# Attention and MLP in one kernel: from interleaved to one after the other, with a pinned order and a division by turned 32x32 blocks

## The chip, the cores and the metric

The kernel runs on one core of a Trainium2 chip. A core has a matrix engine, TensorE (PE, whose weight loads are shown apart as PEld), and four others: VectorE (DVE), ScalarE (ACT), GpSimd (POOL) and SyncE (SP), which here only issues transfers. Each engine works through its own list of instructions in order, and waits on semaphores for the others. PE writes to PSUM, a small memory that DVE and ACT can read; everything else lies in SBUF. The metric is the time of one execution in microseconds, the median of several.

## The reference

```python
batch, n_heads, seq, head_dim = (4, 8, 768, 64)          # attention
q_bits = (np.einsum('bhsd,dk->bhsk', q, proj) > 0)         # 6 hash bits
mask = q_bucket[:, :, :, None] == k_bucket[:, :, None, :]
scores = np.where(mask, scale * np.matmul(q, k.transpose(0, 1, 3, 2)), -1000000000.0)
attn = softmax(scores)            # sum + 1e-09
attn_out = np.matmul(attn, v)     # then (B,H,S,D) -> (B*S, H*D)
h = x @ w_in                      # 3072 x 512 times 512 x 2048
g = np.maximum(h, 0.0) + alpha * np.minimum(h, 0.0)
out = g @ w_out                   # 2048 x 512
```

A query sees only keys with the same six hash bits. A query that no key matches gets the mean of v. q, k and v are float32 and scaled by 0.1; `w_in` and `w_out` are scaled by 1/sqrt(512) and 1/sqrt(2048) and arrive as float64.

## The kernel before, in words

`fast_path` does all the work. After it a flag is read: where the inputs are too large for a softmax without its maximum, `general_path` computes everything again. It is not touched by the change.

Attention goes by *pairs* of heads, 16 in all (4 batches with 4 pairs), because two heads of 64 fill the 128 partitions. A pair has two *units*, one for each half (384) of the queries, so there are 32. A unit consists of:

- `scores` (line 587): for each of six blocks of 128 keys, PE makes a tile `sc` of 128 keys by 2 heads by 384 queries, first the product of the hash bits (bf16), which leaves a large negative number where they differ, then k times q (float32). ACT writes exp of it to a tile `pt` (line 592). Eight `pt` tiles and two `sc` buffers are passed round.
- POOL adds the `pt` tiles up into `acc` (lines 599 and 601): three accumulators with two blocks each in the first four pairs, one with all six blocks later on.
- `attend` (line 608), one unit later: PE multiplies `pt` by v into `av`; ACT copies it to `xT` (line 618).
- `divide` (lines 626 to 634): PE sums `acc` over the keys by a product with ones into `sm`, so that each sum stands in 64 equal rows; DVE takes the maximum with a small number, the reciprocal of all 128x384 elements, the product with `xT`, and POOL adds the mean of v where the sum was empty.

One pair ahead, `turn` transposes q and k on PE (line 550), ACT copies them out, `magnitude` squares them for the flag, and `hash_bits` makes the bits (`hs` on PE, then `qb` and `kb` on DVE).

The weights come as float64 in 32 pieces of 128x512. `round_weight` turns a piece into float32 from its two 32-bit words (lines 530 to 539): Abs on ACT, four operations on DVE, Abs again on ACT, an add on POOL, the sign on DVE. As written, two pieces go with each of the first seven units and four with each one after, until all 32 are done; the scheduler moves their operations ahead where it sees room.

The MLP works on chunks of 384 tokens, two for a batch: `ff1` makes 16 tiles `h` (line 643) whose activation DVE writes to `g` (lines 648 and 650), `ff2` makes three output tiles `z` from 16 products each (line 659), which ACT copies out and SP stores.

What sets the order: one loop over units with four *slots* each. `mlp_slice` puts a thirty-second part of the MLP of a finished batch into each slot, beginning nine units after the batch did:

```python
for u in range(total + UNITS + 2):
    pi, g = divmod(u, NCH)
    live = u < total
    for slot in range(4):
        if live and slot != 1:
            scores(pi, g, (0, None, 1, 2)[slot])
```

So the first eight units stand alone, the next 24 have the MLP of batches 0 to 2 between their matmuls, and the MLP of batch 3 stands alone at the end. Only PE's order is fixed as written (`pe = tc.keep_in_program_order`); the other engines' lists, and SP's, are laid out by the framework's scheduler.

## Time and profile before

| | before |
|---|---|
| median of 3 runs | 1162.95 us (1161.72 to 1164.89) |
| profiled execution | 1162.11 us, span of its instructions 1160.3 us |
| mean granted TensorE clock | 0.971 of full |
| busy: PE / PEld | 1084.9 us (94%) / 510.7 us (44%) |
| busy: DVE / ACT / POOL | 492.9 (42%) / 272.9 (24%) / 325.8 (28%) us |
| read from HBM / written | 35.66 / 6.29 MB |

Busy time is a sum over the whole span; the 40 slices of the page and the table of stretches show where it falls. A float32 matmul shows as two instructions, so 16 of them are 32 rows in a count. In a group's row stand the line, the engine, the operation, what is written and read, the shape, the count, then busy time in us and the mean of one in ns, then the idle time of the engine before it and what ended it. The chain of waits follows the work that ended last back from the end, piece by piece.

### The profile page before, as it was taken

How to read it: one execution, taken by the hardware profiler on the slowest of the kernel's cores; microseconds unless marked ns; L12 is line 12 of the kernel's file. 1: busy time of each engine (PE TensorE's matmuls, PEld its weight loads, DVE VectorE, ACT ScalarE, POOL GpSimd, SP SyncE). 2: the span in 40 equal slices, each digit the busy share in tenths (PEclk: the TensorE clock that was granted, in tenths of full speed). 3: DMA queues.
4: the chain of work that ended last, by engine and by line, in shares of the span. 5: the costliest groups of instructions: out<-in, count | busy, mean ns of one | idle time of the engine just before them, and what ended most of it. 6: DMA issues, size and time to landing. Idle time of an engine off the chain costs nothing.

```text
span 1160.3 us, 10928 instructions
## 1 busy us (share of the span) xinstructions
PE 1084.9 (94%) x4355; PEld 510.7 (44%) x4355; DVE 492.9 (42%) x696; ACT 272.9 (24%) x441; POOL 325.8 (28%) x224
## 2 busy tenths in 40 slices
PE   5676675999999999999999999999999999999997
PEld 3232232454445544454444544455444544554543
DVE  5988988444325430354315430354315421420420
ACT  5445443322222212221222222222221110000000
POOL 3454555422332322323332322223323330000000
PEclk8888787999999999999999999999999999999999
DMA  6434441110010101010010101010000000000000
GB/s 170 120 105 128 122 118 51 41 28 14 13 42 14 28 14 46 23 28 14 10 46 14 28 14 46 24 28 14 10 32 1 1 1 19 10 1 19 9 10 20
DMA packets 62844, 42.75 MB, mean 37 GB/s; under 512 B 51504, under 2 KB 55616, under 8 KB 62784
## 3 DMA queue, kind: packets, MB, share of 16 engines
q1 hardware_dynamic: 62784, 41.96, 12.7%
q8 instruction: 36, 0.59, 0.2%
q14 instruction: 24, 0.20, 0.1%
HBM read 35.66 MB, written 6.29 MB: 36 GB/s over the span
## 4 chain that ended last, share of the span: by engine, by line
PE 82%; DVE 13%; POOL 2%; ACT 1%; issue 1%; DMA 1%; SPq 0%; POOLq 0%; ACTq 0%
PE h L643 29%; PE z L659 29%; PE sc L587 10%; PE av L608 9%; PE sm L626 2%; DVE w_in L539 2%; POOL wr L538 2%; DVE dn L632 1%; PE hs L570 1%; DVE w_out L531 1%; DVE wr L536 1%; DVE w_out L539 1%; DVE w_in L531 1%; DVE wr L535 1%; DVE kb L574 1%; PE tp_k L550 1%
## 5 line engine op out<-in xcount | busy, mean ns | idle before, releaser
L643 PE MATMUL h<-xT,w_in 128*128 128x384 f32 x1024 | 343.5, 489 | 0.0
L659 PE MATMUL z<-w_out,g 128*128 128x512 f32 x768 | 339.0, 595 | 0.0
L601 POOL TENSOR_TENSOR acc<-acc,pt 128x768 f32<-128x768 f32 x96 | 161.0, 1677 | 427.2 <-ACT pt L592 423.4
L643 PEld LDWEIGHTS h<-xT,w_in 128*128 128x128 f32 x1024 | 189.7, 190 | 136.3 <-issue 9.7
L592 ACT ACTIVATE pt<-sc 128x768 f32<-128x768 f32 x192 | 154.7, 810 | 365.8 <-PE sc L587 365.7
L659 PEld LDWEIGHTS z<-w_out,g 128*128 128x128 f32 x768 | 143.2, 190 | 179.7 <-issue 177.3
L648 DVE TENSOR_SCALAR neg<-h,alpha 128x384 f32<-128x384 f32 x128 | 78.9, 617 | 292.9 <-PE h L643 292.7
L587 PE MATMUL sc<-qT,kT 64*128 64x384 f32 x768 | 160.7, 497 | 0.0
L608 PE MATMUL av<-pt,vn 128*64 128x385 f32 x768 | 139.3, 515 | 16.3 <-DVE kb L574 16.3
L599 POOL TENSOR_TENSOR acc<-pt,pt 128x768 f32<-128x768 f32 x48 | 89.9, 1874 | 116.5 <-ACT pt L592 116.5
L630 DVE TENSOR_SCALAR al<-sm,vm 128x384 f32<-128x384 f32 x32 | 19.8, 618 | 218.4 <-PE sm L626 218.2
L608 PEld LDWEIGHTS av<-pt,vn 128*64 128x64 f32 x768 | 55.9, 144 | 94.6 <-issue 94.2
L587 PE MATMUL sc<-qb,kb 64*128 64x384 bf16 x384 | 65.2, 335 | 18.5 <-ACT pt L592 18.4
L632 DVE RECIPROCAL dn<-dn 128x384 f32<-128x384 f32 x32 | 81.6, 2551 | 0.9
L587 PEld LDWEIGHTS sc<-qT,kT 64*128 64x128 f32 x768 | 71.1, 195 | 20.5 <-issue 20.4
L665 ACT COPY o<-z 128x512 f32<-128x512 f32 x24 | 14.0, 585 | 261.7 <-PE z L659 261.7
L650 DVE SCALAR_TENSOR_TENSOR g<-h,neg 128x384 f32<-128x384 f32 x128 | 71.2, 556 | 3.9
L587 PEld LDWEIGHTS <-kb 64*128 64x128 bf16 x384 | 20.5, 94 | 91.2 <-issue 78.5
L570 PE MATMUL hs<-qT,wh 128*32 128x384 f32 x128 | 30.4, 555 | 23.3 <-ACT xT L618 22.6
L618 ACT COPY xT<-av 128x384 f32<-128x384 f32 x32 | 15.2, 474 | 155.9 <-PE av L608 83.4
L634 POOL TENSOR_TENSOR xT<-dn,al 128x384 f32<-128x384 f32 x32 | 32.2, 1007 | 56.3 <-DVE dn L633 56.3
L626 PE MATMUL sm<-acc,ones 128*64 128x384 f32 x192 | 44.1, 574 | 1.2 <-ACT xT L618 1.2
(68 smaller groups left out, 520.2 us busy)
## 6 DMA issues: line engine op xcount, KB each, us to landing
raw<-in_moe_w_in_dram SPq DMA_DIRECT2D x16, 512.0 KB, 3.7
raw<-in_moe_w_out_dram SPq DMA_DIRECT2D x16, 512.0 KB, 3.5
qn<-in_q_dram SPq DMA_DIRECT2D x32, 192.0 KB, 3.4
kn<-in_k_dram SPq DMA_DIRECT2D x32, 192.0 KB, 3.3
vn<-in_v_dram SPq DMA_DIRECT2D x16, 384.0 KB, 3.2
out_dram<-o SPq DMA_DIRECT2D x24, 256.0 KB, 2.0
wh<-in_proj_dram SPq DMA_DIRECT2D x2, 1.5 KB, 2.9
alpha<-in_moe_alpha_dram SPq DMA_DIRECT2D x1, 8.0 KB, 2.2
```

The lines of the kernel that those rows point to most:

```text
L570: pe(nc.tensor.matmul(ps[r : r + 32], wh[s], tr[name, pi][:, cols], start=True, stop=True))
L587: pe(nc.tensor.matmul(sc[:, s, :CW], what["k", pi][r, ks], what["q", pi][r, qs], start=first, stop=not first,))
L592: nc.scalar.activation(pt[:, :, :CW], sc[:, :, :CW], AF.Exp, scale=SCALE)
L599: nc.gpsimd.tensor_tensor(a, prob[pi, g, kc - 1][:, :, :CW], pt[:, :, :CW], op=ALU.add)
L601: nc.gpsimd.tensor_tensor(a, a, pt[:, :, :CW], op=ALU.add)
L608: pe(nc.tensor.matmul(ps[D * s : D * s + D], nat["v", pi][:, s, kc * D : (kc + 1) * D], prob[pi, g, kc][:, s], start=(kc == 0), stop=(kc = ...
L626: pe(nc.tensor.matmul(ps[D * s : D * s + D], ones, a[:, s], start=(i == 0), stop=(i == n - 1)))
L632: nc.vector.reciprocal(den, den)
L643: pe(nc.tensor.matmul(ps, w[:, kk, o : o + P], xT[b][:, kk, ch * CW : (ch + 1) * CW], start=(kk == 0), stop=(kk == NK - 1),))
L648: nc.vector.tensor_scalar(neg, ps, 0.0, alpha[:, f : f + 1], op0=ALU.min, op1=ALU.mult)
L650: nc.vector.scalar_tensor_tensor(g, ps, 0.0, neg, op0=ALU.max, op1=ALU.add)
L659: pe(nc.tensor.matmul(ps, gT[b, ch, f][:, t * P : (t + 1) * P], w_out[part][:, i], start=(f == 0), stop=(f == NF - 1),))
```

## The change

The loop with slots is gone. All 32 units of attention come first, then the eight chunks of the MLP. In detail:

- Every compute instruction of all engines is pinned in program order (`do = tc.keep_in_program_order`); SP's transfers are still placed by the scheduler.
- One weight piece is converted with each unit. It has one Abs fewer (its effect is folded into the constant of the exclusive or), and the upper clamp is replaced by a recorded maximum `wmax`, which the flag tests at the end (weights under 2). The test on q and k is tighter (40 for 60).
- `scores`, `attend` and the adds are taken apart, so that a unit runs: two key blocks, half of the attend of the unit before, two turns or a hash, two key blocks, the other half, two turns or a hash, two key blocks, the sum of the unit before. The first four `pt` tiles are added by POOL (`add_first`), the last two and POOL's result by DVE (`add_last`): one accumulator, two matmuls for `sm`.
- The division turns `sm` by 32x32 blocks on DVE (a transpose within each block), so that the 64 equal rows become columns and one column of each block is enough: 12 columns for the reciprocal, which are spread out again, turned back, and multiplied with `av` straight out of PSUM. The copy of `av` on ACT and the add on POOL are gone; the mean of v for empty sums comes from a small number added on both sides of the fraction.
- The bits of q come from Sign on ACT, those of k from DVE, in one operation.
- The pools of attention are closed before the MLP, which gets four `h` buffers and two `z` buffers in PSUM instead of two for both. The first two `h` tiles of the next chunk are made before `ff2` of a chunk. The flag is computed behind the first chunk's `ff1`.

```diff
-    pe = tc.keep_in_program_order
+    do = tc.keep_in_program_order
...
+    def weight_abs(i):
+        lo, hi = halves(i)
+        do(ACT.activation(piece(i)[0], hi.bitcast(F32), AF.Abs))
+
+    def weight_parts(i):
...
+        wr[i] = r = pool.tile([P, 512], F32, name=f"wr{i}", tag="wr")
+        do(DVE.tensor_scalar(x, x, HI_MIN, None, op0=ALU.max, op1=ALU.max, accum_out=wmax[:, i : i + 1]))
+        do(DVE.tensor_scalar(
+            x.bitcast(U32), x.bitcast(U32), 3, 0xC0000000, op0=ALU.logical_shift_left, op1=ALU.bitwise_xor,
+        ))
+        do(DVE.tensor_scalar(r.bitcast(U32), x.bitcast(U32), 0x7F800000, None, op0=ALU.bitwise_and))
+        do(DVE.scalar_tensor_tensor(r, lo, 2.0 ** -52, r, op0=ALU.mult, op1=ALU.mult))
...
+        do(DVE.tensor_scalar(bits["k", pi][:, cols], ps, tk, mk, op0=ALU.is_gt, op1=ALU.mult))
...
+            do(ACT.activation(bits["q", pi][D * s : D * s + 32, cols], ps[r], AF.Sign, bias=bq[r]))
...
+    def add_first(u, part):
+        p = [prob[u, 2 * part + i][:, :, :CW] for i in range(2)]
+        if part == 0:
+            accp[u] = pool.tile([P, 2, CW], F32, name=f"accp{u}", tag="accp")
+            do(POOL.tensor_tensor(accp[u], p[0], p[1], op=ALU.add))
+        else:
+            for t in p:
+                do(POOL.tensor_tensor(accp[u], accp[u], t, op=ALU.add))
+
+    def add_last(u):
...
+        do(DVE.tensor_tensor(accd[u], p[0], p[1], op=ALU.add))
+        do(DVE.tensor_tensor(accd[u], accd[u], accp[u], op=ALU.add))
...
-        nc.vector.tensor_scalar(alone, ps, EMPTY, vmean[pi], op0=ALU.is_lt, op1=ALU.mult)
-        nc.vector.tensor_scalar(den, ps, EMPTY, None, op0=ALU.max)
-        nc.vector.reciprocal(den, den)
-        nc.vector.tensor_tensor(den, den, x, op=ALU.mult)
-        nc.gpsimd.tensor_tensor(x, den, alone, op=ALU.add)
...
+            do(PE.matmul(ps[D * s : D * s + D], ones, accd[u][:, s], start=True, stop=True))
...
+        do(DVE.transpose(a, ps))
+        do(DVE.tensor_scalar(r, a.rearrange("p (n w) -> p n w", w=32)[:, :, 0], S * EPS, None, op0=ALU.add))
+        do(DVE.reciprocal(r, r))
+        do(DVE.tensor_copy(a.rearrange("p (n w) -> p n w", w=32), r.unsqueeze(2).to_broadcast([P, CW // 32, 32])))
+        do(DVE.transpose(d, a))
+        do(DVE.scalar_tensor_tensor(
+            xT[b][:, hp, g * CW : (g + 1) * CW], av[u][:, :CW], vsum[pi], d, op0=ALU.add, op1=ALU.mult,
+        ))
...
+    for u in range(UNITS + 1):
...
+        if live:
+            scores(u, 0)
+            add_first(u, 0)
+        if u > 0:
+            add_last(u - 1)
+            attend(u - 1, 0)
+        if more:
+            if g == 0:
+                turn(pi + 1, "q", 0)
+                turn(pi + 1, "q", 1)
+            else:
+                hash_bits(pi + 1, 0)
+        if live:
+            weight_parts(u)
+            weight_sum(u)
+            scores(u, 1)
+            add_first(u, 1)
+        if u > 0:
+            attend(u - 1, 1)
...
+        if live:
+            scores(u, 2)
+        if u > 0:
+            divide(u - 1)
+        if live:
+            weight_sign(u)
+            load_weight(u + 3)
+            if u + 1 < NW:
+                weight_abs(u + 1)
+        if more:
+            magnitude(pi + 1, "qk"[g])
...
+    attn.close()
...
+    chunks = [(b, ch) for b in range(B) for ch in range(NCH)]
+    EARLY = 2
+    for n, (b, ch) in enumerate(chunks):
+        for f in range(EARLY if n else 0, NF):
+            ff1(b, ch, f)
+        if n == 0:
             verdict()
...
+        if n + 1 < len(chunks):
+            for f in range(EARLY):
+                ff1(*chunks[n + 1], f)
+        for t in range(CH):
+            ff2(b, ch, t)
```

On PE, in a unit of the interleaved stretch before, `h` products of an earlier batch stand between the score blocks:

```order
L550 MATMUL tp_q_1517<-ident,qn_1280 128x128 x3
L643 MATMUL h_0_7_1522<-xT_344,w_in_82 128x384 x4
L608 MATMUL av_1_1531<-pt_95,vn_940 64x385 x2
L608 MATMUL av_1_1531<-pt_96,vn_940 64x385 x2
L608 MATMUL av_1_1531<-pt_89,vn_940 64x385 x2
L608 MATMUL av_1_1531<-pt_90,vn_940 64x385 x2
L608 MATMUL av_1_1531<-pt_91,vn_940 64x385 x2
L608 MATMUL av_1_1531<-pt_92,vn_940 64x385 x2
L550 MATMUL tp_q_1558<-ident,qn_1280 128x128 x3
L643 MATMUL h_0_8_1563<-xT_344,w_in_83 128x384 x4
L643 MATMUL h_0_9_1572<-xT_344,w_in_83 128x384 x4
```

After the change nothing of the MLP stands there; half an attend and two turns lie between two score blocks, and the sum ends the unit:

```order
L603 MATMUL sc_3_441<-qT_231,kT_262 128x384 x2
L635 MATMUL av_411<-pt_94,vn_156 64x384 x2
L635 MATMUL av_411<-pt_95,vn_156 64x384 x2
L635 MATMUL av_411<-pt_96,vn_156 64x384 x2
L567 MATMUL tp_k_458<-ident,kn_391 128x128 x3
L567 MATMUL tp_k_463<-ident,kn_391 128x128 x3
L603 LDWEIGHTS kb_317
L603 MATMUL sc_4_468<-qb_79,kb_317 128x384
```

All products named h now follow the last sum, so on PE the whole MLP has moved behind the whole of attention.

On DVE in one of the first units before, operations of several weight pieces (`w_in`) stand mixed with a division (`al`, `dn`) and a hash (`qb`, `kb`):

```order
L531 TENSOR_SCALAR w_in_82<-w_in_82 128x512
L571 TENSOR_SCALAR qb_377<-hs_378,tq,cq 128x384
L574 TENSOR_SCALAR kb_80<-hs_378,tk,mk 32x384 x2
L539 SCALAR_TENSOR_TENSOR w_in_82<-raw_374,wr_548 128x512
L630 TENSOR_SCALAR al_0_394<-sm_0_386,vm_342 128x384
L631 TENSOR_SCALAR dn_0_393<-sm_0_386 128x384
L532 TENSOR_SCALAR w_in_82<-w_in_82 128x512
L632 RECIPROCAL dn_0_393<-dn_0_393 128x384
L571 TENSOR_SCALAR qb_377<-hs_414,tq,cq 128x384
L633 TENSOR_TENSOR dn_0_393<-dn_0_393,xT_344 128x384
```

After the change the list of a unit is the same throughout: the two adds (`accd`), a hash, one weight piece, `vs`, a hash, then the division (`st`, `rc`, `dn`):

```order
L624 TENSOR_TENSOR accd_514<-pt_93,pt_94 128x768
L625 TENSOR_TENSOR accd_514<-accd_514,accp_406 128x768
L588 TENSOR_SCALAR kb_524<-hs_525,tk,mk 128x384
L544 TENSOR_SCALAR w_in_80,wmax<-w_in_80 128x512
L545 TENSOR_SCALAR w_in_80<-w_in_80 128x512
L548 TENSOR_SCALAR wr_533<-w_in_80 128x512
L549 SCALAR_TENSOR_TENSOR wr_533<-raw_286,wr_533 128x512
L641 TENSOR_SCALAR vs_559<-av_517 128x1
L588 TENSOR_SCALAR kb_524<-hs_561,tk,mk 128x384
L655 STREAM_TRANSPOSE st_584<-sm_581 128x384
L656 TENSOR_SCALAR rc_585<-st_584 128x12
L657 RECIPROCAL rc_585<-rc_585 128x12
```

The adds have come to DVE, the weight piece stands ahead of the division of the unit before, and nothing of a second piece stands with it.

The flag's transposes on PE (`vd`, two of them) stood before among the last `h` products:

```order
L643 MATMUL h_0_5_4741<-xT_3713,w_in_82 128x384 x4
L643 MATMUL h_0_6_4750<-xT_3713,w_in_82 128x384 x4
L683 MATMUL vd_4762<-ident,top 1x128
L683 MATMUL vd_4765<-ident,top 1x128
L643 MATMUL h_0_7_4771<-xT_3713,w_in_82 128x384 x4
L643 MATMUL h_0_8_4780<-xT_3713,w_in_83 128x384 x4
```

and now, between the first chunk's last `h` and the second chunk's first:

```order
L735 MATMUL h_0_14_3599<-xT_89,w_in_83 128x384 x4
L735 MATMUL h_0_15_3608<-xT_89,w_in_83 128x384 x4
L764 MATMUL vd_3621<-ident,top 1x128
L764 MATMUL vd_3624<-ident,top 1x128
L764 MATMUL vd_3627<-ident,top 1x128
L735 MATMUL h_1_0_3635<-xT_89,w_in_80 128x384 x4
```

They have moved from the end of the program to behind the first chunk, and there are three, which share one buffer.

More of the change, by code (lines that the diff above doesn't have):

```diff
@@ L499, in setup @@
         for t in pts:
-            nc.gpsimd.memset(t[:, :, CW : CW + 1], 1.0)
+            do(POOL.memset(t[:, :, CW : CW + 1], 1.0))
+        for t in qbs:
+            do(POOL.memset(t, 0.0))
     def setup_alpha():
         ps = psum.tile([P, NF], F32, name="alps", tag="mi")
-        nc.tensor.transpose(ps, alpha16, ident[:NF, :NF])
-        nc.vector.tensor_copy(alpha, ps)
-    raw = {}
-    views = [(w_in[j], moe_w_in, j) for j in range(4)] + [(w_out[j], moe_w_out, j) for j in range(4)]
-    def load_weight(i):
-        dst, src, j = views[i // 4]
-        o = i % 4
+        do(PE.transpose(ps, alpha16, ident[:NF, :NF]))
@@ L604, in attend @@
-    def attend(pi, g):
-        ps = psum.tile([P, CW + 1], F32, name=f"av{pi}_{g}", tag="mi")
-        for kc in range(NC):
+            do(ACT.activation(pt[:, :, :CW], sc[:, :, :CW], AF.Exp, scale=SCALE))
+            prob[u, kc] = pt
+    def add_first(u, part):
[6 more added lines that the diff above has]
+                do(POOL.tensor_tensor(accp[u], accp[u], t, op=ALU.add))
@@ L726, in fast_path @@
+    for name in "qkv":
+        load(0, name)
+        if name == "q":
+            setup()
     for name in "qk":
@@ new lines, in fast_path, with ff1 @@
+    attn.close()
+    mpool = ctx.enter_context(tc.tile_pool(name="mlp", bufs=2))
+    mpsum = ctx.enter_context(tc.tile_pool(name="mps", bufs=4, space=bass.MemoryType.PSUM))
+    gT = {}
+    def ff1(b, ch, f):
+        ps = mpsum.tile([P, CW], F32, name=f"h{b}_{ch}_{f}", tag="h", bufs=4)
+        w, o = w_in[f // (NF // 4)], (f % (NF // 4)) * P
+        for kk in range(NK):
+            do(PE.matmul(
+                ps, w[:, kk, o : o + P], xT[b][:, kk, ch * CW : (ch + 1) * CW],
+                start=(kk == 0), stop=(kk == NK - 1),
+            ))
+        neg = mpool.tile([P, CW], F32, name=f"neg{b}_{ch}_{f}", tag="neg")
+        do(DVE.tensor_scalar(neg, ps, 0.0, alpha[:, f : f + 1], op0=ALU.min, op1=ALU.mult))
+        g = mpool.tile([P, CW], F32, name=f"g{b}_{ch}_{f}", tag="g", bufs=NF + 4)
+        do(DVE.scalar_tensor_tensor(g, ps, 0.0, neg, op0=ALU.max, op1=ALU.add))
+        gT[b, ch, f] = g
```

322 lines of the change are left out of this document (126 added, 196 removed).

## The prediction

> **What bounds the kernel now.** I read the page first, then busy time by stretch, then the chain of waits, and last the groups by line. The page's slices show two regimes.
>
> ```profile
> PE   5676675999999999999999999999999999999997
> ...
> DVE  5988988444325430354315430354315421420420
> ...
> PEclk8888787999999999999999999999999999999999
> ```
>
> For seven slices (200 us) PE is busy five to seven tenths at a clock of 0.8, while DVE is nearly full. From the eighth on PE is full, at full clock. Busy time by stretch (the stretch, its length, busy us and instructions of PE, PEld, DVE, ACT and POOL, then clock, DMA share, GB/s) gives the sizes:
>
> ```profile
> 20.00:200.00 180.00, 120.95 (x651) 50.99 (x649) 157.20 (x205) 86.11 (x145) 92.58 (x62) 0.84 0.38 109
> 300.00:860.00 560.00, 560.00 (x2279) 260.50 (x2272) 197.63 (x256) 126.47 (x201) 161.82 (x102) 1.00 0.09 25
> ```
>
> In the first stretch attention stands alone and most weight pieces are converted: PE idles 59 of 180 us and runs at 0.84. In the second PE never idles, so only PE's own work counts there. What can be won lies in the first 200 us. The chain of waits (start, length, work) gives what PE needs for each kind of work at full clock:
>
> ```profile
> 866.97 1.72 PE sc L587 x12
> 868.69 0.48 PE tp_k L550 x3
> ...
> 871.75 4.03 PE av L608 x24
> ...
> 876.26 5.16 PE h L643 x16
> ...
> 883.14 0.78 PE hs L570 x8
> 883.93 5.36 PE h L643 x16
> 889.28 0.80 PE sm L626 x4
> ```
>
> and, from its end, what the MLP needs when it is alone:
>
> ```profile
> 1030.64 41.20 PE z L659 x96
> 1071.84 41.28 PE h L643 x128
> 1113.12 41.21 PE z L659 x96
> ...
> 1154.40 0.58 ACT o L665
> ```
>
> A chunk of the MLP is 41.28 + 41.21 = 82.5 us without a gap.
>
> **The change part by part.** *PE's own work.* A unit (a pair of heads, half of the queries) has three score blocks, an attend and a sum: 3 x 1.72 + 4.03 + 0.80 = 9.99 us. The first unit of a pair now also has the four turns of the next pair, 4 x 0.48 = 1.92: 11.91. The second has its two hashes, 2 x 0.78 = 1.56: 11.55. A pair is 23.46, a unit 11.73 on average. I count unit 0 with the start, and the last pair has nothing to prepare: 15.5 x 23.46 - 1.92 - 1.56 = 360.2 us for 31 units. The MLP is 8 x 82.5 = 660.0, its matmuls being the same. That the first eight units add one accumulator instead of three is inside the 0.80.
>
> *Do the others keep that pace?* The h and z matmuls that covered every other engine are gone from this stage, so all of them must fit into 11.73 us a unit. The groups by line (count | busy us, mean ns | idle before):
>
> ```profile
> L601 POOL TENSOR_TENSOR acc<-acc,pt 128x768 f32<-128x768 f32 x96 | 161.0, 1677 | 427.2 <-ACT pt L592 423.4
> ...
> L592 ACT ACTIVATE pt<-sc 128x768 f32<-128x768 f32 x192 | 154.7, 810 | 365.8 <-PE sc L587 365.7
> ...
> L599 POOL TENSOR_TENSOR acc<-pt,pt 128x768 f32<-128x768 f32 x48 | 89.9, 1874 | 116.5 <-ACT pt L592 116.5
> ...
> L648 DVE TENSOR_SCALAR neg<-h,alpha 128x384 f32<-128x384 f32 x128 | 78.9, 617 | 292.9 <-PE h L643 292.7
> ...
> L538 POOL TENSOR_TENSOR wr<-w_in,wr 128x512 f32<-128x512 f32 x16 | 20.4, 1278 | 30.1 <-DVE wr L536 18.5 <-PE sm L626 7.3 <-DVE vm L614 4.3
> ...
> L551 ACT COPY kT<-tp_k 128x384 f32<-128x384 f32 x32 | 15.2, 478 | 0.0
> ...
> L557 ACT ACTIVATE kn<-kn 128x768 f32<-128x768 f32 x16 | 13.7, 855 | 0.0
> ...
> L530 ACT ACTIVATE w_in<-raw 128x512 f32<-128x512 f32 x16 | 10.6, 665 | 13.1 <-DMA raw<-in_moe_w_in_dram 13.1
> ```
>
> ACT, per unit: six exps at 0.81, two copies at 0.48, a magnitude at 0.86, one Abs at 0.67 (the second is gone), two Signs. A Sign is on no row: nothing below, the 0.86 of the widest other activation above, 0.5 taken since a copy of the same width takes 0.48. Sum 8.3 of 11.73. POOL: 1.87 + 2 x 1.68 + 1.28 = 6.5; its last add of the division is gone. Both fit. The rows of a unit also fit in order: a score block's buffer is free again about 2 us after its matmuls (wait for ACT, then 0.81 for each of two exps), and between two blocks PE has 2.0 us of attend and 0.8 to 1.0 of turns or hashes, or at a unit's end 0.80 of sum, where the first buffer is just free. So I see no stall of that kind, only little slack.
>
> DVE is the tight one. Its groups in the first stretch alone:
>
> ```profile
> L536 DVE SCALAR_TENSOR_TENSOR wr<-raw,wr 128x512 f32<-128x512 uint32 x30 | 20.7, 690 | 0.8
> L539 DVE SCALAR_TENSOR_TENSOR w_in<-raw,wr 128x512 uint32<-128x512 uint32 x16 | 19.1, 1193 | 9.2 <-POOL wr L538 9.0
> L632 DVE RECIPROCAL dn<-dn 128x384 f32<-128x384 f32 x7 | 17.8, 2543 | 0.0
> ...
> L531 DVE TENSOR_SCALAR w_out<-w_out 128x512 f32<-128x512 f32 x16 | 16.9, 1053 | 1.9 <-ACT w_out L530 1.9
> ...
> L532 DVE TENSOR_SCALAR w_out<-w_out 128x512 uint32<-128x512 uint32 x16 | 13.0, 814 | 0.2
> ...
> L535 DVE TENSOR_SCALAR wr<-w_in 128x512 uint32<-128x512 uint32 x15 | 6.4, 424 | 0.4
> ...
> L631 DVE TENSOR_SCALAR dn<-sm 128x384 f32<-128x384 f32 x7 | 3.8, 547 | 0.0
> L633 DVE TENSOR_TENSOR dn<-dn,xT 128x384 f32<-128x384 f32 x7 | 3.8, 545 | 0.0
> ```
>
> L539 is the same kind of work as L536 and takes 0.50 longer; the instructions in order of time show why:
>
> ```profile
> 60.60 2.03 POOL L599 TENSOR_TENSOR acc<-pt,pt 128x768 f32<-128x768 f32 x1
> 60.84 2.33 DVE L539 SCALAR_TENSOR_TENSOR w_in<-raw,wr 128x512 uint32<-128x512 uint32 x1
> ```
>
> The DVE instruction ends 0.54 after POOL's: it stood still while POOL ran. Without such a hold, DVE per unit: the two new adds of 128x768 (L633 and L536 give 1.13 ns a column, so 0.98 each) 1.96; the weight piece 0.55 + 0.42 + 0.42 + 0.69 + 0.69 = 2.77 (the accumulating maximum, on no row, lies between 0.42 and 0.69); a hash 0.62 (as L648). The division falls from 0.62 + 0.55 + 2.54 + 0.55 to two block transposes, two operations on 12 columns, a copy and a product. The transposes are on no row: 0.42 below, 2.54 (a reciprocal of that size) above, 0.55 taken, since L631 also moves 384 columns out of PSUM. The others: 0.2 + 0.2 + 0.45 + 0.55. Division 2.5, unit 7.9. Held back by POOL are the two adds and five weight operations; L539, L531 and L532 lose 0.50, 0.63 and 0.39 on average, so 7 x 0.5 = 3.5. DVE comes to 11.4 of 11.73: level with PE, not past it. The divide of one unit lies behind the weight piece on DVE's order, but PE needs only the adds, which come early in a unit.
>
> The Trainium skill, VectorE: DVE Perf Modes, section "The three transpose paths", gives 311 ns for a DVE transpose of 128x128 in bf16. An estimate from it, three such for 384 columns, is 0.93 a transpose, which would lift DVE to 12.2 and the sum by about 14 us; no run here shows one yet.
>
> *Start, turnover, end.* Before, these rows stand at the start:
>
> ```profile
> 12.34 0.34 PE L587 MATMUL sc<-qb,kb 64*128 64x384 bf16 x2
> ...
> 23.77 0.33 PE L587 MATMUL sc<-qb,kb 64*128 64x384 bf16 x2
> ```
>
> The second row is the first score block of unit 1, so unit 0 ended there. Now the loads of k stand behind proj and alpha on SP's queue, two turns of k are added (0.96, or twice that at half clock), and one raw piece instead of three has to land before the exps. Bounds: 12.34 + 5.16 + 1.92 = 19.4 and 23.8 + 1.9 + 2 = 28. I take 24. The turnover: attend 4.03, sum 0.80, and the sum waits for DVE, which after the previous sum has 2.5 of division, 0.69 and 1.96 to do, 5.2 against 4.03, so some 1.5: 6.3. The verdict now stands on PE between two chunks: the last neg and g (0.62 each at most), then three transposes and three reductions that pass one buffer on, each bounded by 0.55: 2 to 4.5, taken 3.5; it used to run among matmuls that needed nothing of it. The end, from the last z to the span's end, stays 1160.3 - 1154.3 = 6.0. The last weight piece is needed only by z, some 41 us into the MLP, so it hides.
>
> Sum: 24 + 360.2 + 6.3 + 660.0 + 3.5 + 6.0 = 1060. To that a loss per unit: none at best; h in front of sc is 5.36 instead of 5.16, so changes of kind can cost 0.2, and DVE so near PE will sometimes be late, 0.3; 31 x 0.5 = 15.5, together 1075.5. The profiled execution took 1162.11 for a span of 1160.3, and stands 0.8 below the median 1162.95: 1075.5 + 1.8 + 0.8 = **1078 us**, 7.3% less. All rivals below are reckoned from the bare sum, 1060 + 2.6 = 1062.6.
>
> **Rivals.** *DVE becomes the bound.* A transpose of 0.9, an accumulating maximum that pays twice, a little more hold: 13.2 a unit, 31 x (13.2 - 11.73) = 45.6, **1108**. For it: 11.4 is an estimate from means. Against: POOL has four instructions a unit, and can hold DVE once with each.
>
> *The clock sags.* If the attention stage is granted 0.84 as before, 360.2 / 0.84 adds 69 to the forecast: **1147**. For and against stand in these stretches of 4 us:
>
> ```profile
> 84.00:88.00 4.00, 0.56 (x4) 0.00 (x0) 2.53 (x4) 0.63 (x1) 1.88 (x2) 1.00 0.41 122
> 88.00:92.00 4.00, 1.18 (x8) 0.20 (x8) 3.45 (x6) 2.78 (x7) 1.27 (x1) 0.58 0.48 140
> ...
> 108.00:112.00 4.00, 2.77 (x19) 1.36 (x19) 3.13 (x5) 1.46 (x4) 1.76 (x2) 1.00 0.21 40
> ```
>
> After 4 us with PE all but idle the clock is halved; at two thirds busy it is not. I expect nine tenths. The Trainium skill, TensorE: Matmul & The Clock Gate, section "A second HAM failure mode: psum-queue depth-cycling", speaks against the change: small idle gaps while PSUM buffers are passed round made one kernel's clock swing between half and full. By that rule this rival comes true; the row at 108 us does not bear it out.
>
> *Slower than before: the transposes.* If a block transpose costs what the reciprocal of that size does, 2.54, DVE has 11.4 + 2 x 2.0 = 15.4 a unit, and 31 x (15.4 - 11.73) = 114: **1176**. The division would have moved, not shrunk. It decides from 1163 - 1062.6 = 100 us, 3.2 a unit, so from 2.3 us a transpose. Against it: every other DVE row that moves 384 columns once is near 0.55.
>
> *It gains more:* start at the lower bound and no loss per unit, **1058**. *It does not do what it says:* should the new, tighter bound on inputs (40 for 60, weights under 2) be missed, the general path runs behind the fast one and repeats all of PE's work, 1060 more, over **2000**; the weights are scaled by 1/sqrt(512) and 1/sqrt(2048) and q and k by 0.1, so both are far off.
>
> **How the numbers follow.** Forecast (1062 to 1095) 0.61, DVE bound 0.23, clock 0.05, transposes 0.06, more gain 0.04, general path 0.01. The range runs from 1058, the bare sum with the early start, to 1122, DVE at 13.6 a unit; above it lie the tail of the DVE case, the clock, the transposes and the general path, below it next to nothing. What can be told from no change is about 0.3%, 3.5 us. Only the transposes, the general path and the ends of the DVE and clock cases reach there: faster 0.91, same 0.02, slower 0.07.
>
> **What would show it.** Right: PE over 90% busy at a clock near 1.0 until some 390 us, units of 12 to 12.5 us, then chunks of 82.5 us; DVE nine tenths busy in the first stage. A DVE-bound stage would show sm waiting for accd and the chain running over DVE; a sagging clock stands in PEclk; a dear transpose in its own row. I am wrong if the stage takes over 430 us, or if the MLP's chunks are not 82.5.

## The result, and the profile after

The changed kernel takes **1084.97 us** (median of 4 runs, 1084.17 to 1085.34), against 1162.34 for the kernel before in the same comparison: a ratio of 0.933, 95% interval 0.9314 to 0.9346. The forecast was 1078 with a range of 1058 to 1122, so the time lies in the range and the direction was right; the forecast was 7 us too low. The profiled execution has a span of 1082.9 us.

The 40 slices of the changed kernel, the rows that answer to those of before:

```profile
PE   6999999999999998999999999999999999999997
...
DVE  4887888878888794401411410410410420420410
...
PEclk9999999999999998999999999999999999999999
```

The seven slices at five to seven tenths are gone, and with them the clock of 0.8. DVE's work is spread flat over fifteen slices. One dent is left, in the sixteenth slice, where attention hands over to the MLP. By stretch (length, busy us and instructions of PE, PEld, DVE, ACT, POOL, then clock, DMA share, GB/s):

```profile
20.00:200.00 180.00, 172.23 (x1145) 75.63 (x1140) 147.66 (x219) 116.57 (x191) 99.86 (x60) 1.00 0.34 90
200.00:400.00 200.00, 190.89 (x1260) 83.39 (x1258) 166.02 (x253) 128.12 (x206) 106.21 (x64) 1.00 0.29 80
```

In the stretch from 20 to 200 us PE is now busy for 172 instead of 121 us, at full clock. Over the whole span PE's busy time fell from 1084.9 to 1042.6 us and its idle time (span less busy) from 75.4 to 40.3: 42 + 35 us make the 77 of the gain. By groups the sums fell from 44.1 to 28.0 us and the MLP's products `h` and `z`, which stand behind the slow stretch in both kernels, from 682.5 to 664.3 us (groups overlap, so such differences add up to more than 42). How much of the rest is the clock was not taken apart.

Where the gain falls can be read off PE's list. These are the sums of the eighth unit, the kernel before first:

```profile
207.89 0.87 PE L626 MATMUL sm<-acc,ones 128*64 128x384 f32 x4
```

```profile
119.14 0.87 PE L651 MATMUL sm<-accd,ones 128*64 128x384 f32 x4
```

To within one score block the same work lies ahead of both, so some 89 us are won by then, more than the whole gain of 77. Behind it the changed kernel is some 11 us slower than the one before. So the whole gain lies in the first eight units, and behind them the changed kernel, as it stands, wins nothing.

What is still lost in attention is lost at the second unit of each pair, the one with the hashes. The instructions of one such unit in order of time (start, length; in brackets the idle time before and what ended it):

```profile
222.51 0.51 PE L587 MATMUL hs<-kT,wh 128*32 128x384 f32 x1
...
224.07 0.95 DVE L624 TENSOR_TENSOR accd<-pt,pt 128x768 f32<-128x768 f32 x1
...
225.12 0.96 DVE L625 TENSOR_TENSOR accd<-accd,accp 128x768 f32<-128x768 f32 x1
225.99 0.68 DVE L588 TENSOR_SCALAR kb<-hs,tk,mk 128x384 bf16<-128x384 f32 x1
...
226.70 1.16 ACT L591 ACTIVATE qb<-hs,bq 32x384 bf16<-32x384 f32 x2 [5.01 <-DVE kb L588]
...
227.88 1.51 ACT L608 ACTIVATE pt<-sc 128x768 f32<-128x768 f32 x2
...
228.75 0.34 PE L603 MATMUL sc<-qb,kb 64*128 64x384 bf16 x2 [0.79 <-ACT pt L608]
...
231.65 0.34 PE L603 MATMUL sc<-qb,kb 64*128 64x384 bf16 x2 [0.32 <-ACT pt L608]
```

The hash product `hs` begins at 222.51 and takes under a microsecond. DVE reaches `kb`, which reads it, only at 225.99, behind the division, the sign of a weight piece and both adds. The two Signs on ACT read `hs` too and need nothing of `kb`, yet they start only after it: the program names `kb` first, and the two readers of one PSUM tile were put in that order. ACT stands still for 5.01 us, the exps wait behind the Signs on its list, and PE, whose `sc` buffers are passed round by those exps, stops for 0.79 us and, just behind the unit's sum, for 0.32. The waits of the whole run (in total, times, longest) say that this is the rule:

```profile
ACT qb L591 <- DVE kb L588: 78.8, 30, 5.3
...
PE sc L603 <- ACT pt L608: 16.8, 30, 1.0
```

The turnover, in PE's list and in the chain of waits (start, length, work):

```profile
400.24 4.04 PE L635 MATMUL av<-pt,vn 128*64 128x384 f32 x24
408.49 1.18 PE L651 MATMUL sm<-accd,ones 128*64 128x384 f32 x4 [4.20 <-DVE accd L625]
412.56 43.09 PE L735 MATMUL h<-xT,w_in 128*128 128x384 f32 x128 [2.90 <-DVE xT L660]
```

```profile
401.25 0.50 DVE st L655
...
402.89 1.54 DVE st L658
```

PE waits 4.20 us for the last accumulators and 2.90 for the last division. After the first wait the clock is halved (stretches as above):

```profile
408.00:410.00 2.00, 1.18 (x4) 0.20 (x4) 0.73 (x2) 0.00 (x0) 0.00 (x0) 0.73 0.00 0
410.00:412.00 2.00, 0.00 (x0) 0.00 (x0) 1.83 (x6) 0.00 (x0) 0.00 (x0) 0.50 0.00 0
...
416.00:418.00 2.00, 2.00 (x7) 1.15 (x7) 0.98 (x2) 0.00 (x0) 0.00 (x0) 1.00 0.00 0
```

It is back by 416, and the first 128 rows of `h` take 43.1 us instead of 41.28.

### The profile page after: what moved, and what is told of

It is laid out like the page before. It is cut to its first block, busy times and chain, and to the rows that moved or that the text cites. A ratio compares the mean times of both kernels' runs of the same rounds, so it can differ in the third digit from the quotient of the medians.

```text
span 1082.9 us, 10697 instructions
## 1 busy us (share of the span) xinstructions
PE 1042.6 (96%) x4292; PEld 508.9 (47%) x4292; DVE 483.8 (45%) x795; ACT 271.1 (25%) x441; POOL 214.8 (20%) x144
## 4 chain that ended last, share of the span: by engine, by line
PE 78%; DVE 17%; ACT 3%; issue 1%; DMA 0%; SPq 0%; POOL 0%; DVEq 0%; ACTq 0%
PE h L735 31%; PE z L748 30%; PE sc L603 7%; PE av L635 6%; DVE st L658 2%; DVE kb L588 2%; DVE accd L624 2%; DVE accd L625 2%; ACT pt L608 1%; PE sm L651 1%; PE tp_k L567 1%; PE tp_q L567 1%; DVE wr L549 1%; ACT qb L591 1%; DVE xT L660 1%
## 5 line engine op out<-in xcount | busy, mean ns | idle before, releaser
L735 PE MATMUL h<-xT,w_in 128*128 128x384 f32 x1024 | 333.4, 488 | 2.9 <-DVE xT L660 2.9
L635 PE MATMUL av<-pt,vn 128*64 128x385 f32 (+1 forms) x768 | 137.9, 494 | 0.0
L619 POOL TENSOR_TENSOR accp<-accp,pt 128x768 f32<-128x768 f32 x64 | 108.5, 1695 | 2.5
L603 PE MATMUL sc<-qb,kb 64*128 64x384 bf16 x384 | 64.1, 326 | 16.9 <-ACT pt L608 16.8
L616 POOL TENSOR_TENSOR accp<-pt,pt 128x768 f32<-128x768 f32 x32 | 64.5, 2016 | 39.4 <-ACT pt L608 38.6
L591 ACT ACTIVATE qb<-hs,bq 32x384 bf16<-32x384 f32 x64 | 36.6, 573 | 79.4 <-DVE kb L588 78.8
L624 DVE TENSOR_TENSOR accd<-pt,pt 128x768 f32<-128x768 f32 x32 | 54.7, 1710 | 0.0
L658 DVE COPY st<-rc 128x384 f32<-128x384 f32 x32 | 46.3, 1446 | 1.1
L655 DVE STREAM_TRANSPOSE st<-sm 128x384 f32<-128x384 f32 x32 | 18.6, 582 | 54.7 <-PE sm L651 54.7
L552 POOL TENSOR_TENSOR wr<-w_out,wr 128x512 f32<-128x512 f32 x16 | 20.6, 1285 | 76.3 <-DVE vs L641 42.0
L552 POOL TENSOR_TENSOR wr<-w_in,wr 128x512 f32<-128x512 f32 x16 | 20.5, 1282 | 72.3 <-DVE vs L641 41.5
```

The lines of the kernel that those rows point to most:

```text
L591: do(ACT.activation(bits["q", pi][D * s : D * s + 32, cols], ps[r], AF.Sign, bias=bq[r]))
L603: do(PE.matmul(sc[:, s, :CW], what["k", pi][r, ks], what["q", pi][r, qs], start=first, stop=not first,))
L616: do(POOL.tensor_tensor(accp[u], p[0], p[1], op=ALU.add))
L619: do(POOL.tensor_tensor(accp[u], accp[u], t, op=ALU.add))
L624: do(DVE.tensor_tensor(accd[u], p[0], p[1], op=ALU.add))
L635: do(PE.matmul(av[u][D * s : D * s + D, :w], nat["v", pi][:, s, kc * D : (kc + 1) * D], prob[u, kc][:, s, :w], start=(kc == 0), stop=(kc = ...
```

## The experiments

**1. Is it the conversion?** In the kernel before, everything of the conversion but the first Abs on ACT is left out; pieces are still loaded and buffers passed round.

```diff
-        nc.vector.tensor_scalar(dst, dst, HI_MIN, HI_MAX, op0=ALU.max, op1=ALU.min)
...
-        nc.scalar.activation(dst, dst, AF.Abs)
-        nc.gpsimd.tensor_tensor(r, dst, r, op=ALU.add)
```

> The kernel before, with the conversion of the weights left out but for the first Abs on ACT (the loads stay, the output is that of other weights). Theory W, the weights: the attention-only stage of before was slow because the DVE had to convert 32 pieces in it. Then the eight lone units run at PE's pace, some 13 us each with their three accumulators, and about 85 us go: 1075 us (1065 to 1095). Rival C, the cover: attention alone is slow because no h and z stand between its matmuls. Then those units stay above 18 us and the kernel above 1120 us.

Measured 1104.5 us, ratio 0.950 (0.9445 to 0.9555): between the two, 57 us less. Its first stretch:

```profile
20.00:200.00 180.00, 161.96 (x932) 74.91 (x929) 72.69 (x91) 85.89 (x143) 69.76 (x44) 0.97 0.38 117
```

DVE fell from 157 to 73 of 180 us, PE rose from 121 to 162 and the clock came back. The sum of the eighth unit comes at 147.96 us instead of 207.89. So the conversion is most of the early loss, but 18 us of idle PE stay, 10.7 of them before score blocks that wait for an exp and 5.0 before an attend that the trace puts down to `kb`. In the chain of waits of that run DVE's way from `hs` over the old division to the bits returns pair after pair:

```profile
103.51 0.69 DVE kb L562
...
105.35 2.56 DVE dn L620
...
108.00 1.13 DVE dn L621
109.14 0.59 DVE qb L559
109.74 0.67 DVE kb L562
```

**2. The same in the changed kernel.**

```diff
-            weight_parts(u)
-            weight_sum(u)
...
-            weight_sign(u)
```

> The changed kernel with the conversion left out but for the Abs (the output is that of other weights). Per unit DVE loses 3.4 us of 10.1 and POOL 1.3. Theory L, the late hash: what the units lose over PE's bare work (0.6 us on average, all of it in the second unit of a pair) comes from the hash bits being late on DVE, behind the division, the weight piece and the adds; without the piece they come in time and the loss goes: 1085 - 17 - 3 at the turnover = 1065 us (1060 to 1072). Rival P: the loss is PE's own, changes of kind between matmuls: 1080 us or more, only the turnover shorter.

Measured 1069.68 us, ratio 0.9201 (0.9148 to 0.9254): theory L. The spread conversion still costs 15 us. Most of it is the wait of PE for exps, which in this run is 4.6 us instead of 16.8:

```profile
PE sc L604 <- ACT pt L609: 4.6, 15, 0.3
```

The two kernels without conversion differ by 35 us, so the rest of the change (order, one accumulator, bits by Sign, the shorter chain) is worth something of its own in the absence of the conversion; 33 of the 35 are there by the sum of the eighth unit (115.44 against 147.96 us). Which of these carries it was not tried.

**3. The pin undone, PE's order kept.**

```diff
-    do = tc.keep_in_program_order
+    pin = tc.keep_in_program_order
+    def do(x):
+        return x
...
-            do(PE.transpose(ps[:, i * P : (i + 1) * P], src[:, CH * half + i], ident))
+            pin(PE.transpose(ps[:, i * P : (i + 1) * P], src[:, CH * half + i], ident))
```

> The changed kernel with only PE's order pinned, as before; DVE, ACT and POOL are laid out by the scheduler again. Its DVE list draws the weight pieces forward: several pieces stand between two divisions of the first units. Theory W: the first eight or nine units are DVE-bound again (32 x 3.4 us of conversion plus 6.7 us a unit, so some 19 us a unit), the later ones lose their small waits: about 1130 us (1110 to 1150). Rival: the new order on PE is what gains, and the pin only fixes what would come anyway: 1080 to 1090 us.

Measured 1160.04 us, ratio 0.9981 (0.9966 to 0.9996). Not part of the gain is gone but all of it. Stretches of that run:

```profile
20.00:100.00 80.00, 48.94 (x250) 20.14 (x249) 70.04 (x110) 32.31 (x53) 42.98 (x27) 0.74 0.41 122
100.00:200.00 100.00, 64.60 (x328) 26.98 (x329) 81.99 (x137) 41.79 (x68) 46.62 (x29) 0.76 0.33 98
```

This is the picture of before: DVE eight to nine tenths busy until 200 us, PE at two thirds and at a clock of 0.75. The scheduler moves the weight pieces forward again, and the sum of the eighth unit comes at 208.72 us, as in the kernel before. Between two divisions (L662 ends one, L658 begins the next) DVE starts five pieces, of which the first and the last are

```profile
64.46 0.57 DVE L662 STREAM_TRANSPOSE dn<-st 128x384 f32<-128x384 f32 x1
64.95 0.64 DVE L547 TENSOR_SCALAR_CACHE_REDUCE w_in<-w_in 128x512 f32<-128x512 f32 x1
...
83.75 0.68 DVE L547 TENSOR_SCALAR_CACHE_REDUCE w_in<-w_in 128x512 f32<-128x512 f32 x1
...
84.36 0.58 DVE L658 STREAM_TRANSPOSE st<-sm 128x384 f32<-128x384 f32 x1
```

**4. Everything pinned, four pieces in each of the first eight units.** If the pin as such gained, it would still gain here.

```diff
+    def convert(u, n):
+        i = 4 * u + n
+        if i < NW:
+            weight_parts(i)
+            weight_sum(i)
+        if 0 < i <= NW:
+            weight_sign(i - 1)
...
+        convert(u, 0)
...
-            weight_parts(u)
-            weight_sum(u)
```

> The changed kernel, all engines pinned, but four weight pieces with each of the first eight units instead of one with each of 32. It parts the spread from the pin. Theory W: DVE needs 4 x 3.4 + 6.7 = 20 us in each of the first eight units and 6.7 in the rest, so 8 x 8 us are lost and 24 x 0.6 us of waits are won: 1134 us (1115 to 1150). Rival: the pinned order does it, whatever stands in it: under 1095 us.

Measured 1155.28 us, ratio 0.9937 (0.991 to 0.9963):

```profile
100.00:200.00 100.00, 67.69 (x359) 29.49 (x357) 97.30 (x144) 46.68 (x77) 56.71 (x32) 0.83 0.35 111
200.00:300.00 100.00, 98.47 (x652) 42.52 (x652) 55.52 (x84) 62.54 (x100) 45.68 (x25) 1.00 0.21 51
```

Here the sum of the eighth unit comes at 200.29 us. In both runs the loss ends there: from then on a pair takes 23.8 us, less than the 24.7 of the changed kernel.

Runs 3 and 4 together: the new order of PE, the new division and the pin are in one or both of them, and neither keeps more than some 7 of the 77 us. So the gain needs the even spread of one piece per unit, and the pin is needed because it holds the pieces there. That the spread would gain as much without the rest is not shown: no run spreads the conversion in the order of before. There it would also have had less room, since the first chunk of the MLP, which needs all 32 pieces, began at 214 us, and now begins at 412.6. Both came out worse than expected; the rows show a clock of 0.74 to 0.83 beside PE's idle time, which the expectations had not reckoned with.

**5. The division alone undone.** The turned blocks are replaced by a reciprocal of all 384 columns.

```diff
-        do(DVE.transpose(a, ps))
-        do(DVE.tensor_scalar(r, a.rearrange("p (n w) -> p n w", w=32)[:, :, 0], S * EPS, None, op0=ALU.add))
-        do(DVE.reciprocal(r, r))
-        do(DVE.tensor_copy(a.rearrange("p (n w) -> p n w", w=32), r.unsqueeze(2).to_broadcast([P, CW // 32, 32])))
-        do(DVE.transpose(d, a))
+        do(DVE.tensor_scalar(a, ps, S * EPS, None, op0=ALU.add))
+        do(DVE.reciprocal(d, a))
```

> The division by turned blocks is undone alone: the five VectorE operations (turn 0.58, add 0.23, reciprocal of 12 columns 0.23, spread copy 1.45, turn 0.58 us, 3.1 us in all) become an add over 384 columns out of PSUM (0.3 to 0.6) and a reciprocal of all 384 columns (2.55 as in the kernel before), 2.9 to 3.1 us. Theory E (held by GpSimd, the turned blocks cost as much as they save; the gain is the spread of the conversion): 1085 within 5 us. Rival T (the turned blocks carry part of the gain, since a reciprocal of 384 columns can be held too, and the copy is held only where slack is): 31 units with 1 us or more each, 1110 to 1150 us.

Measured 1087.69 us, ratio 0.9363 (0.9329 to 0.9397), which overlaps the interval of the changed kernel: theory E. The groups of both kernels (count | busy us, mean ns | idle before), first the changed one, then this one:

```profile
L658 DVE COPY st<-rc 128x384 f32<-128x384 f32 x32 | 46.3, 1446 | 1.1
L655 DVE STREAM_TRANSPOSE st<-sm 128x384 f32<-128x384 f32 x32 | 18.6, 582 | 54.7 <-PE sm L651 54.7
```

```profile
L656 DVE RECIPROCAL dn<-st 128x384 f32<-128x384 f32 x32 | 81.7, 2553 | 1.1
...
L655 DVE TENSOR_SCALAR st<-sm 128x384 f32<-128x384 f32 x32 | 17.8, 557 | 55.8 <-PE sm L651 55.8
```

0.56 + 2.55 = 3.1 us here; 0.58 + 0.47 + 0.23 + 1.45 + 0.58 = 3.3 us there. One of the things that the title names, the division by turned blocks, thus has no effect on the time that could be measured.

**6. Signs ahead of `kb`.** One line changes its place.

```diff
-        do(DVE.tensor_scalar(bits["k", pi][:, cols], ps, tk, mk, op0=ALU.is_gt, op1=ALU.mult))
         for s in range(2):
...
+        do(DVE.tensor_scalar(bits["k", pi][:, cols], ps, tk, mk, op0=ALU.is_gt, op1=ALU.mult))
```

> Only the place of the two Sign instructions on ScalarE changes: they are issued before VectorE's operation on the same PSUM tile (kb) instead of after it, so they wait for TensorE's hashes and no longer for VectorE, and the exps behind them on ScalarE's list come sooner. Theory Q (the loss of each pair's second unit is a queue on ScalarE: Signs that wait for VectorE's kb hold the exps behind them): the two TensorE gaps of 0.32 and 0.79 us per pair go, 1.11 x 15 pairs = 17 us, 1068 us (1064 to 1074). Rival D (VectorE's own division chain sets the end of the unit, whatever ScalarE's order): 1085, within 4 us either way, and the gaps stand before the exps again with VectorE as what ended them.

Measured 1066.72 us, ratio 0.9179 (0.915 to 0.9208): theory Q, 18.3 us. The same place in that run, and its first stretch:

```profile
215.25 1.16 ACT L590 ACTIVATE qb<-hs,bq 32x384 bf16<-32x384 f32 x2 [1.77 <-PE hs L587]
...
217.79 0.67 DVE L591 TENSOR_SCALAR kb<-hs,tk,mk 128x384 bf16<-128x384 f32 x1
```

```profile
20.00:200.00 180.00, 179.90 (x1202) 76.78 (x1202) 149.21 (x230) 124.33 (x203) 100.12 (x63) 1.00 0.34 93
```

The Signs now wait for PE alone. DVE is as late with `kb` as before, 3.5 us after `hs` began (214.31 us here), and PE no longer notices: no wait for an exp is left in its list. The order of the two readers has turned round: in the whole run `kb` waits 7.0 us for the Signs.

**7. The spread copy on ACT**, which relieves DVE and not ACT's list.

```diff
-        do(DVE.tensor_copy(a.rearrange("p (n w) -> p n w", w=32), r.unsqueeze(2).to_broadcast([P, CW // 32, 32])))
+        do(ACT.copy(a.rearrange("p (n w) -> p n w", w=32), r.unsqueeze(2).to_broadcast([P, CW // 32, 32])))
```

> The copy that spreads the 12 reciprocals over 384 columns goes from VectorE (1.45 us, 0.36 where GpSimd does not hold it) to ScalarE (estimate 0.5 to 0.6, by the Sign of 384 columns, 0.57). Theory D (VectorE's lateness makes the gaps of a pair's second unit): VectorE has 0.9 us less in each chain, most of the 1.11 us per pair goes, 1068 to 1075 us. Theory Q (the queue of ScalarE makes them): the copy stands on the same ScalarE list behind exps and ahead of Signs, and the time stays at 1085 or grows, 1083 to 1100 us.

Measured 1087.69 us, ratio 0.9357 (0.9326 to 0.9388): the time of theory Q. The copy takes 0.51 us on ACT, but ACT waits for its input, and another wait takes the place of the old one:

```profile
ACT st L658 <- DVE rc L657: 52.1, 32, 7.8
...
PE tp_k L567 <- DMA kn<-in_k_dram: 11.0, 10, 2.3
PE sc L603 <- ACT pt L608: 8.6, 26, 1.1
```

PE's waits for exps fall from 16.8 to 8.6 us. In their place it waits 11.0 us for loads of k, which ACT's squares, behind the copy on its list, release late: SP's waits for the squares of q and k grow from 187 to 243 us. So the run does not part the two theories cleanly. Relieving DVE did halve the waits for exps, and the copy put as much back elsewhere on ACT's list. Runs 2 and 8 relieve DVE without burdening ACT, leave the Signs where they are, and bring the same waits down to 4.6 us. What PE loses thus takes both, a late DVE and the Signs that pass its lateness on to the exps; run 6 shows that the order alone cures it.

**8. GpSimd's adds taken out.** One of the changed kernel's readings was that DVE is held by GpSimd.

```diff
-            accp[u] = pool.tile([P, 2, CW], F32, name=f"accp{u}", tag="accp")
-            do(POOL.tensor_tensor(accp[u], p[0], p[1], op=ALU.add))
-        else:
-            for t in p:
-                do(POOL.tensor_tensor(accp[u], accp[u], t, op=ALU.add))
+            accp[u] = p[0]
```

> The changed kernel without GpSimd's three additions per unit: its share of the sums (six of eight key chunks) is left out, and VectorE's second addition takes a tile of exps in their place; all of VectorE's instructions stay. Theory H (VectorE's operations that run beside an operation of GpSimd are held until it ends): the copy that spreads the reciprocals falls from 1.45 us on the mean to 0.36 to 0.5, the first addition (1.71) to about 0.95 to 1.0, while the turns (0.58) stay; with the chain some 1.8 us shorter the 1.11 us per pair go, 1066 to 1070 us. Rival S (the copy is dear in itself, for its broadcast input, and the first addition for two buffers): the durations stay within 10% and the time at 1085 within 4.

Measured 1070.67 us, ratio 0.921 (0.919 to 0.923). Groups between 200 and 400 us of this run, then two of the changed kernel in the same stretch:

```profile
L620 DVE TENSOR_TENSOR accd<-pt,pt 128x768 f32<-128x768 f32 x17 | 16.2, 950 | 0.0
...
L651 DVE STREAM_TRANSPOSE st<-sm 128x384 f32<-128x384 f32 x18 | 10.5, 583 | 53.8 <-PE sm L647 53.8
...
L654 DVE COPY st<-rc 128x384 f32<-128x384 f32 x18 | 6.5, 360 | 0.6
...
L652 DVE TENSOR_SCALAR rc<-st 128x12 f32<-128x12 f32 x18 | 3.1, 173 | 0.6
```

```profile
L624 DVE TENSOR_TENSOR accd<-pt,pt 128x768 f32<-128x768 f32 x17 | 29.2, 1717 | 0.0
...
L656 DVE TENSOR_SCALAR rc<-st 128x12 f32<-128x12 f32 x16 | 7.4, 461 | 0.6
```

What is left out is four of the six `pt` tiles, of which one comes back in DVE's second add (the expectation speaks of six of eight); the add of the weight pieces stays on POOL. Theory H by the durations, with the time just above its range: the copy 1.45 to 0.36 us, the first add 1.72 to 0.95, the operation on 12 columns 0.46 to 0.17, while the turns stay at 0.58. With the copy unheld the whole division, without its last product, is some 1.9 us. PE's waits for exps fall to 4.6 us.

The means hide that the hold is all or nothing. In the changed kernel's trace the first add takes 2.58 us in the 15 cases in which a POOL operation is already running when it starts, and 0.95 in the other 17; the copy 1.56 in 29 cases and 0.36 in three. One of the long ones, with the POOL operation that was ahead of it:

```profile
210.61 2.17 POOL L616 TENSOR_TENSOR accp<-pt,pt 128x768 f32<-128x768 f32 x1 [1.59 <-ACT pt L608]
```

```profile
211.03 2.57 DVE L624 TENSOR_TENSOR accd<-pt,pt 128x768 f32<-128x768 f32 x1
```

It ends 0.82 us after POOL's, as all 15 do.

**9. The turnover filled.** Four of the MLP's first `h` tiles are made while PE waits, and the verdict's transposes stand between products of `ff2`.

```diff
+        if not live:
+            ff1_first(0)
+            ff1_first(1)
         if u > 0:
             divide(u - 1)
+        if not live:
+            ff1_first(2)
+            ff1_first(3)
...
         for t in range(CH):
             ff2(b, ch, t)
+            if n == 0:
+                verdict_turn(t)
```

> The turnover alone: the first four tiles of the MLP's first layer (TensorE 4 x 0.86 us) are made where TensorE waits for the last hash's accumulators and for the last division, into tiles of their own, and the verdict's three turns of a [128,1] column stand between the second layer's products of chunk 0 instead of in one block. Theory L (the 4.20 and 2.90 us of idle at the turnover and the 2.9 of the verdict are on the path, and the halved clock of 420.0 to 426.8 us follows the idle time): -3.4 of TensorE work that now lies under idle time, -1.7 of half clock, -2 to -2.9 of verdict: 7 to 8 us, 1077 us (1074 to 1080). Rival N (what waits is VectorE, whose leaky-ReLU operations of those tiles, 4 x 1 us, now stand ahead of the last division and delay it as much): 1083 to 1087.

Measured 1075.56 us, ratio 0.9256 (0.9227 to 0.9285), 9.4 us less: theory L, by the size of its terms a little more. The halved clock that the expectation puts at 420.0 to 426.8 us stands at 408.9 to 415.7 when time is counted from the span's start, as in the rows of the result; its length is right. Here the stretch of the turnover stays at full clock:

```profile
400.00:430.00 30.00, 28.61 (x105) 15.17 (x102) 20.67 (x37) 1.35 (x2) 4.60 (x3) 1.00 0.00 1
```

**10 and 11. Both together**, with the turned blocks and with the reciprocal of 384 columns (the edits are those of 6 and 9, and of 5 for the second).

> Signs ahead of VectorE's kb and the filled turnover together. Theory A (the two losses are apart from each other, and TensorE is then busy throughout): the gains add, 1162 x (0.9179 + 0.9256 - 0.9334) = 1057 us (1054 to 1061). Rival O (both gains draw on the same slack, as when the Sign's gain makes the turnover start with VectorE later behind): 1062 to 1067.

> As the run before it, and the division by a reciprocal of all 384 columns in place of the turned blocks. In the changed kernel itself that exchange moved the time from 1085 to 1087.7. Theory E (VectorE's chain is still inside TensorE's unit, so its few tenths more don't show, and only the last division of the turnover does, about 1 us): 1057 to 1060. Rival T (with the queue of ScalarE gone the next limit is VectorE's chain, which is longer without the turned blocks): above 1063 us.

Measured 1055.63 us, ratio 0.9084 (0.9069 to 0.9099), and 1056.18, ratio 0.9088 (0.9073 to 0.9103). The gains add, and the division makes no difference here either (the second run came 0.8 us below the range of its theory E). The first of the two from 20 to 1050 us:

```profile
20.00:1050.00 1030.00, 1026.42 (x4221) 495.03 (x4217) 469.96 (x755) 258.93 (x419) 203.61 (x126) 1.00 0.13 38
```

PE idles for under 4 of 1030 us. This version is 29 us faster than the changed kernel; between 20 and 1050 us more can only come from PE's own work. The sum of its eighth unit comes at 113.75 us, and what lies behind that is 13 us shorter than in the kernel before; with the two losses mended the kernel is faster there too.

## Why the prediction was right, and where it was not

| term | predicted | in the trace | difference |
|---|---|---|---|
| start to the end of unit 0 | 24 | 21.24 | -2.8 |
| 31 units, bare 360.2 and loss 15.5 | 375.7 | 379.0 (21.24 to 400.24) | +3.3 |
| turnover | 6.3 | 12.3 (400.24 to 412.56) | +6.0 |
| MLP and verdict | 663.5 | 664.6 (412.56 to 1077.18) | +1.1 |
| end | 6.0 | 5.7 | -0.3 |

- **The bound, right.** The first 200 us were what could be won, as the sums of the eighth unit show, and the MLP's chunks behind the first stayed at 41.28 + 41.20 us. Runs 1, 3 and 4 show that the cause was the conversion's load on DVE in that stretch. (Nine units stand ahead of the first `h` in the kernel before, not eight: the slots begin nine units after the batch.)
- **PE's bare work, right.** In run 6 the sums of three units begin at 209.70, 221.41 and 233.15: a pair takes 23.45 us, where 23.46 was worked out. So the 0.2 us per unit set aside for changes of kind do not exist.
- **The loss per unit, its size nearly right, its reason half right.** 0.5 was taken, 0.61 came (18.8 us over 31 units); that the two are so close is luck, since 0.2 of the 0.5 stood for changes of kind. The other 0.3 stood for a DVE that is sometimes late, and so it is, by runs 2 and 8, but not by the way that was meant. The prediction asked whether each engine's busy time fits into 11.73 us and wrote of the exps "So I see no stall of that kind, only little slack". It did not follow the order on ACT's list: two Signs that wait for DVE stand ahead of exps that could go. Run 6 takes that queue away and with it 18.3 us, with DVE as late as ever.
- **DVE's sum, near, for errors that partly cancel.** 11.4 us a unit were estimated, 10.1 measured (20.2 for a pair). Of the division's operations the transposes were right (0.55 taken, 0.58 measured). The copy was taken at 0.45 and as not held; it takes 1.45, of which 1.09 is the hold (run 8). The hold of 7 x 0.5 us was laid on the adds and the weight operations instead; of these only the first add and the sign of the weights (0.68, or 1.21 on the mean of the 19 cases in which POOL was running) show it on more than one occasion. The others escape because POOL is not running when they start, which the prediction did not ask. The estimate from the Trainium skill's page VectorE: DVE Perf Modes, "The three transpose paths", 0.93 a transpose, is not borne out by the measured 0.58.
- **The turnover, the term mis-sized most.** It counted one wait, for the accumulators, at 1.5 (its own terms, 5.2 against 4.03, give 1.2); this was 4.20, because DVE was still at a weight piece until 401.25, 0.8 us after the previous sum was done, and then took 4.4 instead of 2.5 for the division, with the held copy in it. And it left out that the first `h` needs the last division: 2.90. The 0.4 in the sum and 1.8 in the first `h` are the halved clock, which the prediction's own row ("After 4 us with PE all but idle the clock is halved") would have given, had the wait been seen. Run 9 wins 9.4 us at these places and at the verdict.
- **Rivals.** DVE as the bound did not come: it is busy for 148 of the 180 us from 20 to 200, eight tenths where nine were named as a sign, and run 6 shows PE full beside it. The sagging clock did not come: 1.00 from 20 to 400 us, with 30 stops of up to 1.0 us in the PE list. The rule of the Trainium skill, TensorE: Matmul & The Clock Gate, "A second HAM failure mode: psum-queue depth-cycling", was thus not at work at gaps of this size. The sagging clock's 1147 was reckoned from the forecast; from the bare sum, as the prediction says of all rivals, it is 1131. The dear transpose fell with its row. What the prediction had no word for is the pin: without it the forecast would have been wrong by the whole gain (run 3).

## What to carry to other kernels

Add up each engine's time per unit, but then read each engine's list in order and ask of every instruction whether it waits for a slower engine while others behind it are ready; here two readers of one PSUM tile waited for one another in the order in which the program names them. Work whose due date is far off, such as this conversion, is best laid out in equal portions under a stage that another engine bounds, and it had to be held there, since the scheduler pulled it forward. Where one stage hands over to the next, the last link of its chain is bare: look for work of the next stage that needs only what is ready.

## What the runs showed of the hardware that was not expected

- A DVE operation that starts while a POOL operation is running can be held until that ends: on the mean 0.36 to 1.45 us for a copy, 0.95 to 1.72 for an add of two SBUF tiles, 0.17 to 0.46 for twelve columns. In the changed kernel's trace every held one ended a fixed time after POOL's: 0.82 us the add, 0.55 the sign of a weight piece, 0.22 the copy, 0.03 the twelve columns, each 0.13 to 0.14 less than it takes alone. Where DVE's started first, it was not held: the 13 signs of a weight piece beside which POOL only began took 0.68. The block transposes (0.58), the reciprocals (0.23 and 2.55) and the operation that reads PSUM and makes `kb` (0.67) showed no hold. The Trainium skill, SBUF — State Buffer, "Who interferes with whom", says that copies and `tensor_scalar` operations can contend with GpSimd for a shared port pair, in a mode that uses two ports, and operations with two SBUF inputs beside a GpSimd instruction that reads SBUF, and that the order of issue decides who blocks; the rows of run 8 and the cases counted here agree.
- 4.2 us without PE work were enough to halve the clock for some seven microseconds at the turnover; gaps of up to 1.0 us, two in each pair of 24.7 us and for 380 us on end, left it at 1.00. In run 6 a wait of 4.1 us at the same place halved it for ten.
- A block transpose of 128x384 float32 on DVE takes 0.58 us, out of PSUM or out of SBUF alike.
